# Loads of batch 0 reordered over two queues, later k and v through the Pool queue, and the expansions of k and v moved to chunks 2 and 3

## Chip, cores and metric

One core of one Trainium2 chip. The metric is the time of one execution on the device in microseconds (us), as the median of several runs. The time of a run is some 1.8 us longer than the span of its trace, in which all positions below are given.

## The reference, cut to what matters

```python
# mLSTM cell; 4 batches, 8 heads, 768 steps, head dimension 40
for t in range(S):
    m_new  = np.maximum(f[t] + m, i[t])
    f_stab = np.exp(f[t] + m - m_new);  i_stab = np.exp(i[t] - m_new);  m = m_new
    C = f_stab * C + i_stab * outer(v[t], k[t]);  n = f_stab * n + i_stab * k[t]
    y[t] = sigmoid(o[t]) * (C @ q[t]) / np.maximum(abs(n @ q[t]), 1.0)
x = y.transpose(0, 2, 1, 3).reshape(3072, 320)
# MLP, 320 -> 2048 -> 320
r = np.maximum(x @ w_in, 0.0)
out = (s * (r * r) + b) @ w_out
```

The forget gate is drawn around +3 and is added to the stabilizer m, so the weight of a step falls quickly with its number. The kernel therefore takes k and v of the first 42 steps alone, tests in each execution that this is allowed, and would branch to a full version otherwise.

## The kernel before

The 3072 tokens go in six chunks of 512. Chunk c runs its first MLP layer while the second layer of chunk c-1 runs: sixteen slots of TensorE work, into which "events" are put, that is, small steps of the attention for later chunks. `put(c, slot, step)` places one. Every chunk needs, ahead of it, q and o loaded and q cast and transposed (`qt`); `ps_h`, the state times q; the normalized result `x`; and its transpose `xt`. Chunks 2 to 5 get `qt` and `xt` by DMAs of SyncE, chunks 0 and 1 by TensorE. The state of a batch is `cn`, made from the weighted `kp` (k times the gates) and `v1` (v, cast) through `ps_cn`. The expansions `kbd` and `vbd` are block-diagonal copies of the first 42 steps' k and v, which only chunks 4 and 5 use.

```python
    def load_first(self):                              # cut
        nc.sync.dma_start(out=self.ft, in_=...)        # gates f, i
        nc.sync.dma_start(out=self.it, in_=...)
        ...
        self.load_kv(0, 1, nc.scalar)                  # k, v of batch 0
        self.load_x(0, nc.sync)                        # q, o of chunk 0
        self.load_kv(1, 2, nc.sync)
    def load_rest(self):
        nc.sync.dma_start(out=self.sc, in_=d["s"].partition_broadcast(P))
        nc.sync.dma_start(out=self.bc, in_=d["b"].partition_broadcast(P))
        self.load_kv(2, B, nc.sync)                    # k, v of batches 2 and 3
    def kw(self, bb):                                  # kp = k * gates
        nc.vector.tensor_tensor(out=self.kp[...], in0=self.k32[...], in1=self.at[...], op=ALU.mult)
    def vw(self, bb):                                  # cast of v
        self.nc.gpsimd.tensor_copy(out=self.v1[...], in_=self.v32[...])
    def ev_cn(self, bb):
        ps = self.psB.tile(..., tag="b", name="ps_cn")         # psB: one buffer, shared with ps_h
        ...                                                    # 3 matmuls, then Vector: cn = ps * mask
    def ev_kt(self, bb):
        ps = self.psO.tile(..., tag=self.spare, name="ps_kt")  # psO: one buffer per tag
        ...                                                    # 3 transposes, then Vector: kbd = ps * mask
    def ev_vr(self, bb):
        ps = self.psO.tile(..., tag=self.spare, name="ps_vr")
        ...                                                    # 3 matmuls, then Vector: vbd = ps * mask
    def start(self):                                   # cut
        self.warm(34); self.gates(); self.kw(0); self.warm(10)
        self.qcast(0, 0, nc.vector); self.qcast(0, 1, nc.scalar)
        self.ev_cn(0); self.warm(16)
        self.ev_q(0, 0); self.ev_q(0, 1, nc.vector, early=True); self.warm(12)
        self.tanh(0, 0); self.ev_h(0, 0, early=True); ...
```

`warm(n)` issues n matmuls of ones whose only purpose is to keep TensorE busy.

Of the kernel before, what the change touches and what calls it, by code (L numbers as in the profile page):

```python
# [16 lines left out]
P = 128  # L17
L = 42
# [13 lines left out]
class Short:  # L32
# [30 lines left out]
    def load_first(self):  # L63
        nc, c, d = self.nc, self.const, self.d
        self.ft = c.tile([BH, L], F32, name="ft")
        self.it = c.tile([BH, L], F32, name="it")
        nc.sync.dma_start(out=self.ft, in_=d["f"].rearrange("b h s -> (b h) s")[:, 0:L])
        nc.sync.dma_start(out=self.it, in_=d["i"].rearrange("b h s -> (b h) s")[:, 0:L])
        self.k32 = c.tile([L, BH, D], F32, name="k32")
        self.v32 = c.tile([L, BH, D], F32, name="v32")  # L70
        self.x32 = {}
        self.wi = self.keep.tile([P, 2, DFF], BF16, name="wi")
        self.wr = self.keep.tile([P, NF // 4, 2 * P], BF16, name="wr")
        self.wo = self.keep.tile([P, NF, DM], BF16, name="wo")
        self.sc = self.keep.tile([P, 1], F32, name="sc")
        self.bc = self.keep.tile([P, 1], F32, name="bc")
        self.fa = c.tile([P, S // 4], F32, name="fa")
        self.ia = c.tile([P, S // 4], F32, name="ia")
        self.load_kv(0, 1, nc.scalar)
        self.load_x(0, nc.sync)  # L80
        self.load_kv(1, 2, nc.sync)

    def load_rest(self):
        nc, d = self.nc, self.d
        nc.sync.dma_start(out=self.sc, in_=d["s"].partition_broadcast(P))
        nc.sync.dma_start(out=self.bc, in_=d["b"].partition_broadcast(P))
        self.load_kv(2, B, nc.sync)

    def load_rest2(self):
        nc, d = self.nc, self.d  # L90
# [116 lines left out]
        nc.vector.tensor_copy(out=self.tri, in_=ps)  # L207


    def kw(self, bb):  # L210
        nc = self.nc
        nc.vector.tensor_tensor(
            out=self.kp[0:L, bb, 0:H, :],
            in0=self.k32[:, bb * H : (bb + 1) * H, :],
            in1=self.at[:, bb * H : (bb + 1) * H].unsqueeze(2).to_broadcast([L, H, D]),
            op=ALU.mult,
        )
# [305 lines left out]
    def events(self):  # L523

        e = {}

        def put(c, at, step, *args):
            e.setdefault((c, at), []).append(lambda: step(*args))

        v, a = self.nc.vector, self.nc.scalar  # L530
        put(0, 0, self.qcast, 1, 0, v)
        put(0, 0, self.qcast, 1, 1, v)
        put(0, 3, self.square, 0, 0, 0)
        put(0, 4, self.ev_q, 1, 0, v)
        put(0, 4, self.ev_q, 1, 1, v, True)
        put(0, 5, self.tanh, 1, 0)
        put(0, 6, self.ev_h, 1, 0)
        put(0, 6, self.square, 0, 0, 1)
        put(0, 7, self.tanh, 1, 1)
        put(0, 10, self.ev_x, 1, 0)  # L540
        put(0, 10, self.ev_h, 1, 1)
        for n in range(2, 8):
            put(0, 9 + min(n, 6), self.square, 0, n // 2, n % 2)
        put(0, 15, self.ev_x, 1, 1)
        put(0, 15, self.bias, 0, 8)
        put(1, 0, self.make_tri)
        put(1, 1, self.kw, 2)
        put(1, 1, self.bias, 8, NF)
        put(1, 3, self.load_rest2)
        for c in range(2, 6):  # L550
            d = c - 1

            q0, r0, t0, h0, y0, q1, r1, t1, h1, y1 = {
                2: (4, 5, 6, 8, 10, 5, 6, 8, 11, 13),
                3: (-7, -6, 0, 1, 4, -6, -5, 2, 5, 8),
            }.get(c, (-11, -10, 0, 1, 4, -10, -9, 2, 5, 8))
            for at, step in (
                (q0, lambda c=c: self.qcast(c, 0, a)),
                (r0, lambda c=c: self.tr_q(c, 0)),
                (t0, lambda c=c: self.tanh(c, 0)),  # L560
                (h0, lambda c=c: self.ev_h(c, 0)),
                (y0, lambda c=c: self.tr_x(c, 0)),
                (q1, lambda c=c: self.qcast(c, 1, a)),
                (r1, lambda c=c: self.tr_q(c, 1)),
                (t1, lambda c=c: self.tanh(c, 1)),
                (h1, lambda c=c: self.ev_h(c, 1)),
                (y1, lambda c=c: self.tr_x(c, 1)),
            ):
                put(d + at // 16, at % 16, step)
            if c >= B:  # L570
                put(d - 1, 14, self.ev_s, c, 0)
                put(d, 3, self.ev_s, c, 1)
        put(1, 3, self.ev_cn, 2)
        put(1, 3, self.kw, 3)
        put(1, 6, self.ev_cn, 3)
        put(1, 2, self.ev_kt, 0)
        put(1, 4, self.ev_vr, 0)
        put(1, 7, self.ev_kt, 1)
        put(1, 9, self.ev_vr, 1)
        put(2, 9, self.ev_kt, 2)  # L580
        put(2, 10, self.ev_vr, 2)
        put(2, 11, self.ev_kt, 3)
        put(2, 12, self.ev_vr, 3)
        put(1, 14, self.load_y, 0, self.nc.sync)
        put(2, 10, self.load_y, 2, self.nc.sync)
        put(2, 1, self.flag_a)
        put(2, 3, self.flag_b)
        put(2, 7, self.flag_c)
        put(3, 9, self.flag_d)
        return e  # L590

    def start(self):

        nc = self.nc
        self.load_first()
        self.masks()
        self.vw(0)
        self.load_wi(0)
        self.load_wi(1)
        self.load_x(1, nc.gpsimd)  # L600
        self.vw(1)
        self.load_wi(2)
        self.load_wi(3)
        self.masks_late()
        for k in range(4):
            self.load_wo(k)
        self.load_rest()
        self.load_x(2, nc.gpsimd)
        self.vw(2)
        self.vw(3)  # L610
        self.load_x(3, nc.gpsimd)
        self.ps_w = self.psO.tile([P, 512], F32, tag="o0", name="ps_w")
        self.warm(34)
        self.gates()
        self.kw(0)
        self.warm(10)
        self.qcast(0, 0, nc.vector)
        self.qcast(0, 1, nc.scalar)
        self.ev_cn(0)
        self.warm(16)  # L620
        self.ev_q(0, 0)
        self.ev_q(0, 1, nc.vector, early=True)
        self.warm(12)
        self.tanh(0, 0)
        self.ev_h(0, 0, early=True)
        self.tanh(0, 1)
        self.ev_h(0, 1, early=True)
        self.warm(40)
        self.ev_x(0, 0)
        self.warm(14)  # L630

    def run(self):
        nc, tc = self.nc, self.tc
        with tc.manual_schedule():
            self.start()
            prev = None
            at = self.events()
            for c in range(6):
                for k in range(4):
                    self.spare = f"o{(k + 1) % 2}" if c > 0 else "o1"  # L640
                    if c > 0:
                        self.mm1_rem(c, k, 0)
                        self.mm1_rem(c, k, 1)
                    elif k == 0:
                        self.kw(1)
                        for a in range(2):
                            self.mm1_rem(0, 0, a, 0, N // 2)
                            self.mm1(0, 0, a, 0, N // 2)
                            if a == 0:
                                self.ev_x(0, 1)  # L650
                        self.ev_cn(1)
                        self.warm(8)
                    for a in range(2):
                        if c == 0:
                            n0 = N // 2 if k == 0 else 0
                            self.mm1_rem(c, k, a, n0)
                            self.mm1(c, k, a, n0)
                        else:
                            self.mm1(c, k, a)
                        if c > 1 or (k, a) > (0, 0) and c > 0:  # L660
                            self.square(*prev)
                        self.relu(c, k, a)
                        prev = (c, k, a)
                        for n, (f0, f1) in enumerate((((0, 3), (3, 6)), ((6, 11), (11, 16)))[a]):
                            for e in at.pop((c, 4 * k + 2 * a + n), []):
                                e()
                            if c > 0:
                                self.mm2(c - 1, k, f0, f1)
                if c == 3:
                    self.asked = nc.values_load(self.flag[0:1, 0:1], min_val=0, max_val=1)  # L670
            assert not at
            self.square(*prev)
            for tb in range(CT):
                self.mm2(5, tb, 0, NF, pool="h")
# [218 lines left out]
```

## Time and profile before

| | |
|---|---|
| median of 3 runs | 145.23 us (144.66 to 146.41) |
| span of the profiled run | 143.4 us |
| mean granted clock of TensorE | 0.991 of full speed |
| first real matmul (`hp<-xt,wr`) | 13.27 us |
| length of chunks 0, 1, 2, 3, 4 | 16.60, 23.12, 20.22, 19.14, 18.96 us |
| chunk 5 and the last second layer | 26.94 us |

The length of a chunk is the distance between the starts of the first `hp<-xt,wr` matmuls of two successive chunks, read from the timeline of TensorE. Chunk 4 has no trouble at 18.96 us, chunk 1 takes 4.16 us longer.

One row of the page is the clock granted in 40 equal slices of the span (a 9 is 90% or more of full speed). The clock's records in this trace begin at 4.15 us, and the row and the mean count the time before them as full; the warm-up matmuls of that time took about 100 ns each, against 60 ns later:

```profile
PEclk9999999999999999999999999999999999999996
```

### The profile page before, as it was taken

How to read it: one execution, taken by the hardware profiler on the slowest of the kernel's cores; microseconds unless marked ns; L12 is line 12 of the kernel's file. 1: busy time of each engine (PE TensorE's matmuls, PEld its weight loads, DVE VectorE, ACT ScalarE, POOL GpSimd, SP SyncE). 2: the span in 40 equal slices, each digit the busy share in tenths (PEclk: the TensorE clock that was granted, in tenths of full speed). 3: DMA queues.
4: the chain of work that ended last, by engine and by line, in shares of the span. 5: the costliest groups of instructions: out<-in, count | busy, mean ns of one | idle time of the engine just before them, and what ended most of it. 6: DMA issues, size and time to landing. Idle time of an engine off the chain costs nothing.

```text
span 143.4 us, 2633 instructions
## 1 busy us (share of the span) xinstructions
PE 133.4 (93%) x1009; PEld 78.9 (55%) x1009; DVE 91.7 (64%) x195; ACT 68.3 (48%) x85; POOL 20.7 (14%) x47
## 2 busy tenths in 40 slices
PE   7998999999999949999999999999999999999950
PEld 7796643456555526547555645565555454557730
DVE  6769748996769954998748984569943535244120
ACT  3362479753579316655247663465355343550000
POOL 6994959300000000000000000000000000000000
PEclk9999999999999999999999999999999999999996
DMA  3999999999151789977992365011341110111211
GB/s 50 322 189 284 263 207 197 266 314 286 54 113 46 150 169 186 176 158 160 189 200 68 97 120 139 9 50 40 63 101 46 48 48 0 46 46 46 96 51 59
DMA packets 43336, 18.45 MB, mean 129 GB/s; under 512 B 33396, under 2 KB 42452, under 8 KB 43316
## 3 DMA queue, kind: packets, MB, share of 16 engines
q1 hardware_dynamic: 37576, 11.38, 36.0%
q0 software_dynamic: 4896, 6.56, 20.9%
q10 hardware_dynamic: 844, 0.27, 0.8%
q8 instruction: 10, 0.16, 0.5%
q14 instruction: 10, 0.08, 0.2%
HBM read 13.75 MB, written 3.93 MB: 123 GB/s over the span
## 4 chain that ended last, share of the span: by engine, by line
PE 69%; DVE 5%; DMA 2%; issue 0%; SPq 0%; DVEq 0%
PE o L454 27%; PE hp L419 24%; PE hp L407 7%; PE o2t L454 6%; DMA xt<-x 2%; PE ps_h L337 1%; DVE fac L360 1%; DVE x L365 1%; PE ps_b L441 1%; DVE osb L460 1%; PE ps_kt L241 1%; PE ps_s L315 0%; DVE g L433 0%; DVE rec L358 0%; PE ps_vr L256 0%
## 5 line engine op out<-in xcount | busy, mean ns | idle before, releaser
L426 ACT ACTIVATE r<-hp 128x1024 bf16<-128x1024 f32 x48 | 49.0, 1024 | 51.4 <-PE hp L419 49.7
L454 PE MATMUL o<-wo,g 128*128 128x320 bf16 x320 | 52.6, 299 | 0.0
L419 PE MATMUL hp<-xt,wi 128*128 128x512 bf16 (+1 forms) x200 | 49.9, 372 | 0.0
L454 PEld LDWEIGHTS <-g 128*128 128x128 bf16 x384 | 36.3, 98 | 17.9 <-DVE fm L506 0.3
L433 DVE TENSOR_TENSOR g<-r 128x1024 bf16<-128x1024 bf16 x48 | 32.3, 683 | 10.7 <-ACT r L426 10.6
L419 PEld LDWEIGHTS <-wi 128*128 128x128 bf16 x200 | 17.1, 98 | 22.8 <-issue 9.8
L460 DVE SCALAR_TENSOR_TENSOR osb<-o,sc,brep 128x320 f32<-128x320 f32 x20 | 10.9, 545 | 11.2 <-PE o L454 11.0
L407 PE MATMUL hp<-xt,wr 64*128 64x512 bf16 (+1 forms) x100 | 15.6, 373 | 2.5 <-DMA xt<-x 1.8
L360 DVE SCALAR_TENSOR_TENSOR fac<-th,rec 128x640 f32<-128x640 f32 x12 | 10.5, 876 | 1.8 <-ACT th L294 0.8
L521 PE MATMUL ps_w<-ones 128*128 128x128 bf16 x134 | 10.1, 239 | 1.1 <-POOL ones L134 1.1
L365 DVE TENSOR_TENSOR x<-ps_h,fac 128x640 bf16<-128x640 f32 x12 | 9.9, 824 | 0.4
L521 PEld LDWEIGHTS <-ones 128*128 128x128 bf16 x134 | 9.1, 109 | 1.1 <-POOL ones L134 1.1
L454 PE MATMUL o2t<-wo,g 128*128 128x320 bf16 x64 | 8.9, 299 | 0.0
L407 PEld LDWEIGHTS <-wr 64*128 64x128 bf16 x100 | 3.5, 94 | 9.6 <-issue 9.0
L294 ACT ACTIVATE th<-ox 128x640 f32<-128x640 f32 x8 | 5.7, 728 | 0.5 <-DMA ox<-in_o_gate_dram 0.5
L460 DVE SCALAR_TENSOR_TENSOR osb<-o2t,sc,brep 128x320 f32<-128x320 f32 x4 | 2.2, 550 | 5.9 <-PE o2t L454 5.9
L378 ACT COPY xt<-ps_x 128x768 bf16<-128x768 bf16 x4 | 3.2, 796 | 4.0 <-PE ps_x L376 4.0
L288 ACT CAST qb<-qx 128x480 bf16<-128x480 f32 (+1 forms) x10 | 4.0, 456 | 2.1 <-DMA qx<-in_q_dram 2.1
L337 PE MATMUL ps_h<-cn,qt 120*128 120x123 bf16 (+1 forms) x60 | 4.8, 212 | 0.1
L350 DVE TENSOR_SCALAR d<-ps_h 128x16 f32<-128x16 f32 x8 | 1.4, 170 | 5.0 <-PE ps_h L337 5.0
L337 PEld LDWEIGHTS <-qt 120*128 120x128 bf16 x60 | 3.7, 98 | 1.1 <-issue 0.4
L119 POOL DMA_DIRECT2D wi<-in_moe_w_in_dram x4 | 3.1, 764 | 2.2 <-DMA wi<-in_moe_w_in_dram 2.1
(91 smaller groups left out, 82.7 us busy)
## 6 DMA issues: line engine op xcount, KB each, us to landing
out_dram<-osb SPq DMA_DIRECT2D x23, 160.0 KB, 2.0
qx<-in_q_dram POOLq DMA_DIRECT2D x3, 640.0 KB, 9.4
ox<-in_o_gate_dram POOLq DMA_DIRECT2D x3, 640.0 KB, 10.6
wo<-in_moe_w_out_dram POOLq DMA_DIRECT2D x4, 320.0 KB, 7.1
qy<-in_q_dram SPq DMA_DIRECT2D x8, 160.0 KB, 3.7
oy<-in_o_gate_dram SPq DMA_DIRECT2D x8, 160.0 KB, 3.8
wi<-in_moe_w_in_dram POOLq DMA_DIRECT2D x4, 256.0 KB, 7.9
qx<-in_q_dram SPq DMA_DIRECT2D x1, 640.0 KB, 4.5
```

The lines of the kernel that those rows point to most:

```text
L288: eng.copy(out=out, in_=in_)
L294: self.nc.scalar.activation(out=th, in_=self.src("o", c, i), func=ACT.Tanh, scale=0.5)
L337: nc.tensor.matmul(ps[:, j, g * 123 : g * 123 + w], lhsT=lhs, rhs=rhs[:, g, :, :].rearrange("k a e -> k (a e)")[:, 0:w], start=True, stop= ...
L360: nc.vector.scalar_tensor_tensor(out=fac, in0=self.th.pop((c, i))[:, :, :, :].rearrange("p j h d -> p (j h) d"), scalar=1.0, in1=rec[:, :] ...
L365: nc.vector.tensor_tensor(out=x[:, :, 0:DM].rearrange("p j (h d) -> p j h d", h=H), in0=hv[:, :, :, 0:D], in1=fac[:, :, :].rearrange("p (j ...
L407: nc.tensor.matmul(hp[:, e, n0:n1], lhsT=self.wr[64 * e : 64 * e + 64, k, a * P : (a + 1) * P], rhs=self.xt[64 * e : 64 * e + 64, t0:t1, 2 ...
L419: nc.tensor.matmul(hp[:, e, n0:n1], lhsT=self.wi[:, kt, f * P : (f + 1) * P], rhs=self.xt[:, t0:t1, kt, :], start=False, stop=(kt == 1),)
L426: self.nc.scalar.activation(out=r1, in_=self.hp.pop((c, k, a)), func=ACT.Relu)
L433: self.nc.vector.tensor_tensor(out=self.g[c][:, f : f + 3 : 2, :], in0=r1, in1=r1, op=ALU.mult)
L454: nc.tensor.matmul(self.o2[c, tb][:], lhsT=self.g[c][:, f, tb * P : (tb + 1) * P], rhs=self.wo[:, f, :], start=(f == 0), stop=(f == NF - 1),)
L460: nc.vector.scalar_tensor_tensor(out=osb, in0=self.o2.pop((c, tb)), scalar=self.sc[:, 0:1], in1=self.brep, op0=ALU.mult, op1=ALU.add)
L521: self.nc.tensor.matmul(self.ps_w[:, 0:P], lhsT=self.ones[:], rhs=self.ones[:], start=True, stop=True)
```

## The change

The intent: issue q and o of chunk 0 first, by moving the gates to Scalar's queue, where k and v of batch 0 already are; take k, v of batches 2 and 3 out of the crowded early transfers, into GpSimd's (Pool) queue; give their `kp` to GpSimd; spread the expansions, `ps_tri` and chunk 2's preparation so that Vector is free in chunk 1 and `xt` of chunk 2 is ready in time; use fewer warm-up matmuls.

```diff
-        nc.sync.dma_start(out=self.ft, ...)
-        nc.sync.dma_start(out=self.it, ...)
+        nc.scalar.dma_start(out=self.ft, ...)
+        nc.scalar.dma_start(out=self.it, ...)
     ... load_rest:
-        nc.sync.dma_start(out=self.sc, ...)
-        nc.sync.dma_start(out=self.bc, ...)
-        self.load_kv(2, B, nc.sync)
+        nc.gpsimd.dma_start(out=self.sc, ...)
+        nc.gpsimd.dma_start(out=self.bc, ...)
+        self.load_kv(2, B, nc.gpsimd)
     ... kw(self, bb, eng): eng.tensor_tensor(...) in place of nc.vector.tensor_tensor(...)
     ... events:
-        put(1, 0, self.make_tri)
-        put(1, 1, self.kw, 2)
-                2: (4, 5, 6, 8, 10, 5, 6, 8, 11, 13),
+                2: (3, 4, 5, 6, 9, 3, 4, 7, 9, 12),     # q cast, qt, tanh, ps_h, xt; twice
-        put(1, 3, self.ev_cn, 2)
-        put(1, 3, self.kw, 3)
-        put(1, 6, self.ev_cn, 3)
-        ... ev_kt and ev_vr of batches 0 and 1 at slots 2, 4, 7, 9 of chunk 1,
-            of batches 2 and 3 at slots 9 to 12 of chunk 2
+        put(1, 2, self.ev_cn, 2)
+        put(1, 7, self.ev_cn, 3)
+        put(2, 9, self.make_tri)
+        for bb, k0, v0 in ((0, 6, 7), (1, 10, 11), (2, 6, 8), (3, 10, 12)):
+            put(2 + bb // 2, k0, self.ev_kt, bb)        # batches 0, 1 in chunk 2; 2, 3 in chunk 3
+            put(2 + bb // 2, v0, self.ev_vr, bb)
     ... start:
-        self.warm(34)
+        self.warm(24)
-        self.kw(0)
-        self.warm(10)
+        self.kw(0, nc.vector)
+        self.kw(2, nc.gpsimd)
+        self.kw(3, nc.gpsimd)
+        self.warm(8)
-        self.warm(16)
-        self.ev_q(0, 0)
-        self.ev_q(0, 1, nc.vector, early=True)
-        self.warm(12)
+        self.warm(6)
+        self.ev_q(0, 0, nc.vector)
+        self.ev_q(0, 1, early=True)
+        self.warm(9)
```

After the change, line numbers from 211 to about 540 are smaller by one: L407 before is L406 after, and so on.

More of the change, by code (lines that the diff above doesn't have):

```diff
@@ L66, in load_first @@
         self.it = c.tile([BH, L], F32, name="it")
-        nc.sync.dma_start(out=self.ft, in_=d["f"].rearrange("b h s -> (b h) s")[:, 0:L])
-        nc.sync.dma_start(out=self.it, in_=d["i"].rearrange("b h s -> (b h) s")[:, 0:L])
+        nc.scalar.dma_start(out=self.ft, in_=d["f"].rearrange("b h s -> (b h) s")[:, 0:L])
+        nc.scalar.dma_start(out=self.it, in_=d["i"].rearrange("b h s -> (b h) s")[:, 0:L])
         self.k32 = c.tile([L, BH, D], F32, name="k32")
@@ L84, in load_rest @@
         nc, d = self.nc, self.d
-        nc.sync.dma_start(out=self.sc, in_=d["s"].partition_broadcast(P))
-        nc.sync.dma_start(out=self.bc, in_=d["b"].partition_broadcast(P))
-        self.load_kv(2, B, nc.sync)
+        nc.gpsimd.dma_start(out=self.sc, in_=d["s"].partition_broadcast(P))
+        nc.gpsimd.dma_start(out=self.bc, in_=d["b"].partition_broadcast(P))
+        self.load_kv(2, B, nc.gpsimd)
     def load_rest2(self):
@@ L207, in make_tri, with kw @@
         nc.vector.tensor_copy(out=self.tri, in_=ps)
-    def kw(self, bb):
-        nc = self.nc
-        nc.vector.tensor_tensor(
+    def kw(self, bb, eng):
+        eng.tensor_tensor(
             out=self.kp[0:L, bb, 0:H, :],
@@ L572, in events @@
                 put(d, 3, self.ev_s, c, 1)
-        put(1, 3, self.ev_cn, 2)
-        put(1, 3, self.kw, 3)
-        put(1, 6, self.ev_cn, 3)
-        put(1, 2, self.ev_kt, 0)
-        put(1, 4, self.ev_vr, 0)
-        put(1, 7, self.ev_kt, 1)
-        put(1, 9, self.ev_vr, 1)
-        put(2, 9, self.ev_kt, 2)
-        put(2, 10, self.ev_vr, 2)
-        put(2, 11, self.ev_kt, 3)
-        put(2, 12, self.ev_vr, 3)
+        put(1, 2, self.ev_cn, 2)
[4 more added lines that the diff above has]
+            put(2 + bb // 2, v0, self.ev_vr, bb)
         put(1, 14, self.load_y, 0, self.nc.sync)
@@ L644, in run @@
                     elif k == 0:
-                        self.kw(1)
+                        self.kw(1, nc.vector)
                         for a in range(2):
```

## The prediction

> **What bounds the kernel now.** I read the page first: busy shares, the chain that ended last, the costliest groups.
>
> ```profile
> PE 133.4 (93%) x1009; PEld 78.9 (55%) x1009; DVE 91.7 (64%) x195; ACT 68.3 (48%) x85; POOL 20.7 (14%) x47
> PE 69%; DVE 5%; DMA 2%; issue 0%; SPq 0%; DVEq 0%
> ```
>
> TensorE is the bound, and Vector has 50 us to spare on average. So the change can gain only TensorE's idle time, and loses wherever it makes TensorE wait. The list of waits names one sizeable wait of TensorE after the start:
>
> ```profile
> PE hp L407 <- DMA xt<-x: 1.8, 1, 1.8
> ```
>
> The chain in order of time shows where it sits, at the border of chunks 1 and 2. (Chunks 0 to 5 have 16 slots each: four groups k, whose slots are 4k to 4k+3; a group's last matmuls of the second layer stand in slot 4k+3.)
>
> ```profile
> 48.14 0.83 DVE x L365
> ...
> 49.19 0.47 DVE osb L460
> ...
> 49.68 0.40 SPq L472
> 50.08 0.05 issue
> 50.13 2.73 DMA xt<-x
> 52.86 0.14 issue
> 52.99 0.61 PE hp L407 x4
> ```
>
> Chunk 2's second x is ready at 49.2, but SyncE first sends group 2's output, which waits for osb; the transpose lands at 52.86. From 52.99 to 138.3 the chain is TensorE alone, but for stretches too short to see: every wait added there lengthens the kernel in full. Before chunk 1 there is the start: the first real matmul (L407) runs at 13.27, the rest is filled with warm-up matmuls.
>
> A third reading decides my prediction: how long a PSUM tile stays occupied. Pool psB has one buffer for ps_h and ps_cn; psO has one buffer per tag, and ps_kt, ps_vr, ps_fl of one group share the tag that the group's output does not use. The timelines of Vector and of TensorE in chunk 1:
>
> ```profile
> 44.50 0.82 DVE L365 TENSOR_TENSOR x<-ps_h,fac 128x640 bf16<-128x640 f32 x1
> 45.47 0.46 PE L337 MATMUL ps_h<-cn,qt 120*128 120x123 bf16 x6
> ```
>
> The second ps_h starts 0.15 us after Vector's last read of the first one (45.32): the buffer is already the limit there. And in chunk 2 Vector runs late, after two rounds of normalization and the flags:
>
> ```profile
> 60.73 0.16 DVE L350 TENSOR_SCALAR d<-ps_h 128x16 f32<-128x16 f32 x1
> ...
> 63.31 0.68 DVE L433 TENSOR_TENSOR g<-r 128x1024 bf16<-128x1024 bf16 x1
> 63.91 0.41 DVE L503 TENSOR_REDUCE fm<-ps_fl 1x2 f32<-1x256 f32 x1
> ```
>
> ```profile
> 61.24 0.84 PE L454 MATMUL o<-wo,g 128*128 128x320 bf16 x5
> 61.92 0.38 PE L498 MATMUL ps_fl<-idf,fl 128*1 128x128 f32 x2
> 62.37 0.85 PE L454 MATMUL o<-wo,g 128*128 128x320 bf16 x5
> ```
>
> TensorE writes ps_fl at 61.92, Vector reads it 2 us later, and nobody minds, since nothing reuses that buffer soon. That changes.
>
> [...] q of chunk 0 moves from 2.8 to 5.4 us, o from 5.4 to 7.7. [...] The first 34 warm-up matmuls take 3.52 us (about 100 ns each), 40 later ones 2.40 (60 ns)[...].
>
> **The change part by part.**
>
> *Start.* q and o are issued at 0.8 instead of 1.73 us, so they land some 0.9 earlier (about 5.3 and 7.9; now Scalar gets q at 6.28 and o at 8.84). But ft, it, k0, v0 all go through Scalar's queue, which delays its table load (1.28 us, now from 1.86) by about 0.9: the exponential starts near 4.1 instead of 3.84, a at 5.2, kp at 5.75. Vector's cast of q follows kp, 5.75 to 6.5 instead of 6.28 to 7.01. Then transposes, copy (now 0.56 on Vector), the 9 warm-ups, ps_h near 8.4 instead of 8.52; reciprocal and tanh end near 9.5 instead of 9.69. The chain of Vector behind it is unchanged, so the gain is about 0.2 us, not 0.9. Fewer warm-ups leave TensorE idle near 3.5 to 4.5[...]: gain between -0.8 and +1.0.
>
> *Transfers in the Pool queue.* 1344 packets of k and v leave the crowded stretch of 12 to 19 us and stand behind wo. I expect v near 26 to 30, casts, two more loads (0.93 each), then kw(2) and kw(3): kp(2) near 30 to 33.5. TensorE wants it at slot 2 of chunk 1, near 34. It fits, tightly: 0.2 us for the risk.
>
> *Chunk 1* (times from its first matmul, 29.87 before). TensorE loses ps_tri, two ps_kt, two ps_vr: 0.06 + 4 x 0.17 = 0.74 us less work. New waits: (a) ev_h(2,0) stands at slot 6, reached at 9.1. Its qt comes by a transpose that SyncE issues after group 0's output, near 7.05, and 3.0 later (39.31 to 42.3 now) it is there: 10.05, a wait of 1.0. (b) ev_cn(3), which stood before both ev_h, now stands at slot 7, 0.68 us after ps_h(2,0), and needs the same psB buffer; Vector frees it 2.5 + 0.15 us after ps_h's end: a wait of 1.95. These 2.95 us take the place of 1.84 (xt) and 0.3 (psB at 45.47). TensorE ends chunk 1 at 20.99 - 0.74 + 2.95 = 23.2; the last xt arrives between 23.1 and 23.7, as chunk 3's transposes still precede it on SyncE. Before: 23.12. So the wait for xt that the change attacks is bought back by two others: 0.0 to +0.6, taken as +0.4.
>
> *Chunk 2.* ps_kt(0) stands at slot 6, ps_vr(0) and ps_fl at slot 7, all three on one buffer, and the instruction order of the changed kernel has Vector's kbd behind ev_h(3,1) and a square. In times of now: ps_kt at 61.40, 0.68 of output matmuls, ps_vr wanted at 62.25; kbd starts at 63.91 where the reduction stands today, 0.53 long, so ps_vr at 64.5: a wait of 2.25. ps_vr 0.17, its vbd 0.25 later and 0.55 long, so ps_fl at 65.4: a wait of 0.73. Another 0.2 at slot 11. Work: +0.34 in group 1, and 0.40 for 0.62 in group 2, and 0.17 less in group 3. Sum 3.18 + 0.34 - 0.22 - 0.17 = +3.1.
>
> *Chunk 3.* Four expansions at 0.17 and a wait of 0.2 for group 1's osb, which kbd now precedes: +0.9.
>
> Sum: -0.2 + 0.2 + 0.4 + 3.1 + 0.9 = +4.4. Taken a little smaller, since Vector's backlog may be shorter than I carry over: +3.8, so 149.0 us.
>
> **Rivals.**
> 1. *The change does what it intends*: Vector is freed in chunk 1, xt comes a slot earlier, the start gains all of 0.9. For it: the 1.84 us wait and the 0.74 us of work moved. Against it: the moved work returns on TensorE, and one buffer each in psB and psO. Time: 145.23 - 1.84 - 0.9 = 142.5 at best, not quite 2%.
> 2. *GpSimd becomes the bound in chunk 1*: v lands late, kp(2) after 34. For it: its DMA issues already wait for landings (2.06 us before wi at 14.30) and DMA is about full until 36. Against it: 672 of the 160 B packets took 1.6 us on Scalar's queue. It would add 1 to 3 us to the sum, 150 to 152.
> 3. *The waits I find shrink*: the wait of chunk 1 at slot 7 only replaces the later wait for xt, and Vector reaches kbd sooner in chunk 2. Then +1 to +2: 146.2 to 147.2.
>
> **Range and chances.** The parts range from -0.8 to +1.0 at the start, -0.5 to +1.5 in chunk 1, +2.0 to +3.5 in chunk 2, +0.6 to +1.0 in chunk 3. Not all fall on one side, so 146.8 to 150.6. 2% slower is 148.13, 0.9 below my value: slower 0.70. Rival 3, or a full gain at the start, gives "same": 0.26. Over 2% faster would take more than all of TensorE's idle time after the start: 0.04.
>
> **What would show each step.** In the waits of the changed kernel: ps_vr, or L453 behind it, waiting for Vector's kbd, some 2 us, and ps_fl for vbd, 0.7 us, both in group 1 of chunk 2; ps_cn waiting about 2 us for Vector's x in chunk 1; ps_h waiting about 1 us for qt; the wait for xt under 0.6. First L406 matmul near 13.1. Kp's two multiplies on GpSimd[...] done by 33.5. I am wrong if TensorE passes slot 7 of chunk 2 without idling, if the first real matmul comes before 12.5, or if ps_cn(2) waits for GpSimd.

## More of the kernel before

Repeated runs of the kernel before lie between 144.6 and 146.9 us, but for one of 159.86 at a mean clock of 0.849. Those with a recorded clock fall into two groups: a mean of 0.989 or more took 144.59 to 145.88 us, a mean of 0.979 to 0.981 took 146.39 to 146.85. No trace of the second group was kept.

## The result, and the profile after

The changed kernel took 159.2 us (median of 4 runs, 158.95 to 160.32) against 145.09 us in the same rounds: a ratio of 1.097, with a 95% interval of 1.088 to 1.106. A ratio here and below is the mean time of one kernel's fast runs over that of the other's in the same rounds, so it is not quite the ratio of the medians quoted. The direction was predicted, the size was not: +3.8 us predicted, some +14 measured, and 159 is far outside the range.

The page of the changed kernel, its busy shares, clock row and chain:

```profile
PE 138.7 (88%) x984; PEld 80.3 (51%) x984; DVE 90.8 (58%) x193; ACT 68.3 (43%) x85; POOL 26.0 (17%) x53
PEclk9999999999995999995599999999999999999999
PE 57%; DMA 13%; DVE 10%; POOL 10%; issue 4%; ACTq 1%; SPq 1%; ACT 0%; DVEq 0%; POOLq 0%
```

TensorE has 25 instructions fewer than before and is yet busy 5.3 us longer. That points to a slower clock: three slices show a 5 where the row of before has only nines up to its last slice. TensorE's part of the chain fell from 69% to 57%: transfers, Vector and GpSimd now hold a third of the span, against 7% before.

Chunk by chunk, from the timelines of TensorE (us):

| | before | after | difference |
|---|---|---|---|
| first real matmul | 13.27 | 17.30 | +4.03 |
| chunk 0 | 16.60 | 16.40 | -0.20 |
| chunk 1 | 23.12 | 26.38 | +3.26 |
| chunk 2 | 20.22 | 26.19 | +5.97 |
| chunk 3 | 19.14 | 19.96 | +0.82 |
| chunk 4, chunk 5 and tail | 45.90 | 45.91 | 0 |
| sum | | | +13.88 |

From the list of waits after, those that matter here (total, number, longest, in us):

```profile
POOL v L219 <- DMA v<-in_v_dram: 9.7, 2, 5.4
PE ps_vr L255 <- DVE kbd L244: 2.3, 1, 2.3
PE ps_cn L225 <- DVE x L364: 2.0, 1, 2.0
PE ps_cn L225 <- POOL v L219: 2.0, 1, 2.0
DVE nm L184 <- DMA it<-in_i_gate_dram: 1.9, 1, 1.9
PE ps_h L336 <- DMA qt<-qb: 0.8, 1, 0.8
PE ps_fl L497 <- DVE vbd L260: 0.7, 1, 0.7
PE hp L406 <- DMA xt<-x: 0.6, 1, 0.6
PE ps_cn L225 <- POOL kp L211: 0.5, 1, 0.5
```

Five of these are the predicted waits, close to their predicted sizes (predicted in brackets): 2.26 for `kbd` (2.25), 1.96 for Vector's `x` (1.95), 0.82 for `qt` (1.0), 0.71 for `vbd` (0.73), 0.64 for `xt` (under 0.6). Four were not in the sum: the waits for the transfers of v and `it` and for the cast of v belong to the start, and `kp` is what the prediction named as its way to be wrong.

**The start.** The cast of v of batch 0 and the matmuls behind it, before:

```profile
3.88 0.45 POOL L220 CAST v<-v 42x320 bf16<-42x320 f32 x1 [0.36 <-DMA v<-in_v_dram]
5.58 0.38 PE L226 MATMUL ps_cn<-v,kp 128*120 128x123 bf16 x3
```

and after (start, duration, engine and line; in brackets the idle time before it and what ended it):

```profile
8.95 0.45 POOL L219 CAST v<-v 42x320 bf16<-42x320 f32 x1 [5.43 <-DMA v<-in_v_dram]
9.45 0.47 PE L225 MATMUL ps_cn<-v,kp 128*120 128x123 bf16 x3 [1.96 <-POOL v L219]
17.30 0.28 PE L406 MATMUL hp<-xt,wr 64*128 64x256 bf16 x2
```

v is usable 5 us later, `ps_cn(0)` starts 3.87 us later, and the first real matmul follows 4.03 us later. GpSimd issues the weight loads and everything else of its queue behind that cast, so all of it is late as well: the first load of `wi` is issued at 9.35 us in place of 4.28.

**The Pool queue and the two new waits of chunk 1.** TensorE after:

```profile
38.59 0.38 PE L225 MATMUL ps_cn<-v,kp 128*120 128x123 bf16 x3 [0.55 <-POOL kp L211]
40.26 0.61 PE L406 MATMUL hp<-xt,wr 64*128 64x512 bf16 x4
44.33 0.47 PE L336 MATMUL ps_h<-cn,qt 120*128 120x123 bf16 x6 [0.82 <-DMA qt<-qb]
47.45 0.48 PE L225 MATMUL ps_cn<-v,kp 128*120 128x123 bf16 x3 [1.96 <-DVE x L364]
49.19 1.04 PE L406 MATMUL hp<-xt,wr 64*128 64x512 bf16 x4
```

The last line is the surprise. The same four matmuls take 0.61 us at 40.26 and 1.04 us at 49.19, after the 1.96 us wait. The windows of the trace show why (window, its length, busy time of TensorE with the number of its instructions, of its weight loads, of Vector, Scalar and GpSimd, then the granted clock, the share of DMA and GB/s). Their borders are those of the clock's own changes, which lie 3.413 us or a multiple of it apart in the traces (in this one at 13.38, 47.51, 50.92, 71.40 and 78.23 us), and so on a grid of 3.413 us:

```profile
44.10:47.51 3.41, 1.22 (x12) 0.80 (x13) 2.43 (x6) 1.10 (x2) 0.00 (x0) 1.00 0.29 56
47.51:50.92 3.41, 3.41 (x14) 1.21 (x15) 1.72 (x4) 0.00 (x0) 0.00 (x0) 0.50 0.07 23
67.99:71.40 3.41, 1.34 (x11) 0.83 (x9) 3.19 (x7) 2.01 (x5) 0.00 (x0) 1.00 0.74 163
71.40:74.82 3.42, 2.52 (x12) 1.04 (x11) 1.23 (x4) 0.00 (x0) 0.00 (x0) 0.50 0.31 62
74.82:78.23 3.41, 3.41 (x12) 1.14 (x12) 1.15 (x2) 0.41 (x1) 0.00 (x0) 0.50 0.44 106
```

A window in which TensorE is busy only 1.22 of 3.41 us (0.36) is followed by one at half clock; the same at 67.99 (0.39), which holds most of the predicted 2.26 us wait for `kbd`. There the clock stays at half for a second window; the first one at half clock was busy 0.74. The windows from 47.51 and 74.82, busy 1.00, were each followed by full clock. This is the wait, with the Vector instruction that ended it:

```profile
71.00 0.54 DVE L244 TENSOR_TENSOR kbd<-ps_kt,bdm 120x378 bf16<-120x378 bf16 x1
71.59 0.47 PE L255 MATMUL ps_vr<-v,sel 128*126 128x123 bf16 x3 [2.26 <-DVE kbd L244]
```

The wait for `xt` of the kernel before is nearly as long (1.84 us), but a border of the grid cuts it in two: the windows that hold its halves are busy 0.77 and 0.69, and no half clock follows either:

```profile
48.52:51.94 3.42, 2.63 (x18) 1.44 (x15) 3.05 (x7) 1.68 (x2) 0.00 (x0) 1.00 0.82 178
51.94:55.35 3.41, 2.35 (x19) 1.33 (x20) 0.43 (x2) 0.74 (x1) 0.00 (x0) 1.00 0.95 167
```

So three theories had to be tested: the start is late because of the loads and not because of fewer warm-ups; two waits cost their length and half a clock window or more on top; and the Pool queue delays `kp(2)`.

### The profile page after: what moved, and what is told of

Its sections match the earlier page's. It is cut to its first block, busy times and chain, and to the rows that moved or that the text cites. A ratio compares the mean times of both kernels' runs of the same rounds, so it can differ in the third digit from the quotient of the medians.

```text
span 157.1 us, 2583 instructions
## 1 busy us (share of the span) xinstructions
PE 138.7 (88%) x984; PEld 80.3 (51%) x984; DVE 90.8 (58%) x193; ACT 68.3 (43%) x85; POOL 26.0 (17%) x53
## 3 DMA queue, kind: packets, MB, share of 16 engines
HBM read 13.75 MB, written 3.93 MB: 113 GB/s over the span
## 4 chain that ended last, share of the span: by engine, by line
PE 57%; DMA 13%; DVE 10%; POOL 10%; issue 4%; ACTq 1%; SPq 1%; ACT 0%; DVEq 0%; POOLq 0%
PE o L453 23%; PE hp L418 18%; PE hp L406 6%; PE o2t L453 6%; DMA wi<-in_moe_w_in_dram 5%; DMA v<-in_v_dram 4%; DVE fac L359 2%; DVE x L364 2%; DVE g L432 2%; DMA qt<-qb 2%; DMA xt<-x 2%; POOL qx L103 2%; POOL ox L103 2%; PE ps_h L336 1%; DVE osb L459 1%
## 5 line engine op out<-in xcount | busy, mean ns | idle before, releaser
L453 PE MATMUL o<-wo,g 128*128 128x320 bf16 x320 | 53.9, 306 | 0.0
L418 PE MATMUL hp<-xt,wi 128*128 128x512 bf16 (+1 forms) x200 | 51.1, 379 | 0.0
L453 PEld LDWEIGHTS <-g 128*128 128x128 bf16 x384 | 37.0, 99 | 18.6 <-issue 0.5
L432 DVE TENSOR_TENSOR g<-r 128x1024 bf16<-128x1024 bf16 x48 | 32.9, 694 | 12.7 <-ACT r L425 12.6
L406 PE MATMUL hp<-xt,wr 64*128 64x512 bf16 (+1 forms) x100 | 16.4, 392 | 1.3 <-DMA xt<-x 0.6
L359 DVE SCALAR_TENSOR_TENSOR fac<-th,rec 128x640 f32<-128x640 f32 x12 | 9.9, 825 | 1.8 <-ACT th L293 0.8
L520 PEld LDWEIGHTS <-ones 128*128 128x128 bf16 x109 | 8.5, 119 | 1.1 <-POOL ones L134 1.1
L406 PEld LDWEIGHTS <-wr 64*128 64x128 bf16 x100 | 3.5, 95 | 9.0 <-issue 7.1
L225 PE MATMUL ps_cn<-v,kp 128*120 128x123 bf16 x12 | 1.7, 260 | 4.5 <-DVE x L364 2.0
L230 DVE TENSOR_TENSOR cn<-ps_cn,bdm 120x369 bf16<-120x369 f32 x4 | 2.2, 546 | 3.8 <-PE ps_cn L225 3.8
```

Source lines behind the costliest of these rows:

```text
L359: nc.vector.scalar_tensor_tensor(out=fac, in0=self.th.pop((c, i))[:, :, :, :].rearrange("p j h d -> p (j h) d"), scalar=1.0, in1=rec[:, :] ...
L406: nc.tensor.matmul(hp[:, e, n0:n1], lhsT=self.wr[64 * e : 64 * e + 64, k, a * P : (a + 1) * P], rhs=self.xt[64 * e : 64 * e + 64, t0:t1, 2 ...
L418: nc.tensor.matmul(hp[:, e, n0:n1], lhsT=self.wi[:, kt, f * P : (f + 1) * P], rhs=self.xt[:, t0:t1, kt, :], start=False, stop=(kt == 1),)
L432: self.nc.vector.tensor_tensor(out=self.g[c][:, f : f + 3 : 2, :], in0=r1, in1=r1, op=ALU.mult)
L453: nc.tensor.matmul(self.o2[c, tb][:], lhsT=self.g[c][:, f, tb * P : (tb + 1) * P], rhs=self.wo[:, f, :], start=(f == 0), stop=(f == NF - 1),)
L520: self.nc.tensor.matmul(self.ps_w[:, 0:P], lhsT=self.ones[:], rhs=self.ones[:], start=True, stop=True)
```

## The experiments

All gave correct results. "First real" is the start of the first real matmul. Ratios are to the kernel before in the same rounds; the changed kernel was not run again in them, so differences to it cross rounds. By the rule of 2% the record calls `gates_only`, `warm_only`, `fill_waits` and `gates_held` unclear; what is read from them are positions in one profiled run each. How far such positions scatter: in the changed kernel and in the three runs that keep its loads and warm-ups (4, 6, 7), first real lies between 17.30 and 17.78.

**1. `undo_gates`: the changed kernel with the gates back on SyncE.**

```diff
-        nc.scalar.dma_start(out=self.ft, ...); nc.scalar.dma_start(out=self.it, ...)
+        nc.sync.dma_start(out=self.ft, ...);   nc.sync.dma_start(out=self.it, ...)
```

> The changed kernel with the loads of both gates back on SyncE's queue, ahead of q and o; all else as changed. Theory (queue order at the start: with the gates gone, q and o start first and fill the DMA engines, so that it, k and v of batch 0 land 3 to 5 us late and hold the exponential, kp, ps_cn and GpSimd's queue): the first real matmul comes back from 17.3 to about 13.3 us and the time falls by 4 us, to about 155. Rival (the 25 warm-up matmuls that were taken out leave TensorE cold, and that makes the start late): the first real matmul stays at 16 us or later, time 158 to 159.

Measured: 154.92 us (152.42 to 155.21). First real 14.31, against 17.30; cast of v at 4.00. The runs split by clock (0.960 to 0.967, and 0.983 in the fastest), so no ratio is quoted; the borders of the chunks are the evidence. The gates' queue was worth 3.0 us of the start. What remains over 13.27 may belong to the clock: the trace has a half-clock window from 7.71 to 11.13, and `all_mended` below, with the same queue for the gates and the same warm-ups, had none and started at 12.79.

**2. `gates_only`: the kernel before with only the gates moved to Scalar's queue.**

```diff
-        nc.sync.dma_start(out=self.ft, ...);   nc.sync.dma_start(out=self.it, ...)
+        nc.scalar.dma_start(out=self.ft, ...); nc.scalar.dma_start(out=self.it, ...)
```

> The kernel before with only the two gate loads moved from SyncE's to Scalar's queue. Theory of the queue order: first real matmul near 17 us instead of 13.3, v of batch 0 cast on GpSimd near 9 us, time +4 us, about 149. Rival of the cold clock: with the 34 warm-ups kept, no more than +1 us.

Measured: 150.64 us, ratio 1.037 (1.031 to 1.044). First real 18.24; chunks 1 to 5 are those of before to 0.03 us. Two lines of the change alone cost 4.97 us of the start, with all the old warm-ups in place. The cast of v waits for its transfer:

```profile
9.39 0.45 POOL L220 CAST v<-v 42x320 bf16<-42x320 f32 x1 [5.87 <-DMA v<-in_v_dram]
```

**3. `warm_only`: the kernel before with only the new warm-up counts and the swapped copies of qt.**

```diff
-        self.warm(34) ... warm(10) ... warm(16) ... warm(12)
+        self.warm(24) ... warm(8)  ... warm(6)  ... warm(9)
-        self.ev_q(0, 0); self.ev_q(0, 1, nc.vector, early=True)
+        self.ev_q(0, 0, nc.vector); self.ev_q(0, 1, early=True)
```

> The kernel before with only the fewer warm-up matmuls (24, 8, 6, 9 for 34, 10, 16, 12) and the two copies of transposed q exchanged between Vector and Scalar. Theory of the queue order: within 1 us of before. Rival of the cold clock: the granted clock comes up later than 4.2 us and the first real matmul is 2 us or more later.

Measured: 145.56 us, ratio 1.001 (0.991 to 1.011). First real 14.08, with half clock from 7.33 to 10.74, but chunk 0 then takes 16.06 in place of 16.60, and chunk 1 begins only 0.27 later. With the fewer warm-ups the clock fell in this trace (in `all_mended`, with the same warm-ups, it did not), and it cost next to nothing: the first chunk takes the delay up. What limits it instead, perhaps its transfers, was not tested.

**4. `fill_waits`: the changed kernel, TensorE kept busy in two of the waits** by matmuls with a matrix of zeros into the open sum of the output.

```diff
+    def fill(self, c, tb, n):
+        for _ in range(n):
+            self.nc.tensor.matmul(self.o2[c, tb][:], lhsT=self.zero[:], rhs=self.wo[:, 0, :], start=False, stop=False)
+        put(1, 7, self.fill, 0, 1, 14)     # ahead of ps_cn(3)
+        put(2, 7, self.fill, 1, 1, 16)     # ahead of ps_vr(0)
+        put(2, 7, self.fill, 1, 1, 5)      # ahead of ps_fl
```

> The changed kernel with matmuls by a zero matrix added to an open output sum, 14 ahead of ps_cn of batch 3 in chunk 1, 16 ahead of ps_vr and 5 ahead of ps_fl in chunk 2: TensorE works through the waits, and what it waits for is untouched. The result is the same. Theory (a stretch in which TensorE idles lets the clock fall to half for one or two windows of 3.4 us): the two half-clock stretches at 47.5 and 71.4 go, chunk 1 gets 1.5 us shorter and chunk 2 3 us shorter, total about 154.5. Rival (the waits alone cost the time, the half clock falls on work that has slack or has another cause): the time stays at 159, within 1 us.

Measured: 155.13 us, ratio 1.071 (1.062 to 1.079), so 4.1 us less than the median of the changed kernel, for *more* work on TensorE. The two windows that had been followed by half clock are now busy 0.88 and 0.96, and the clock is at 1.00 from 13.32 us to the end of the work:

```profile
44.03:47.45 3.42, 3.00 (x25) 2.07 (x25) 2.25 (x5) 1.30 (x2) 0.00 (x0) 1.00 0.30 58
67.93:71.34 3.41, 3.29 (x26) 2.07 (x24) 2.63 (x6) 0.86 (x3) 0.00 (x0) 1.00 0.88 94
```

Chunk 1 goes from 26.38 to 24.79 (-1.59), chunk 2 from 26.19 to 23.57 (-2.62). The sum, 4.21 us, is the price of the half clock; the waits themselves are still there, filled: counted from the start of their chunk, `ps_cn(3)` starts after 13.74 us (13.75 in the changed kernel) and `ps_vr(0)` after 11.51 us in both.

**5. `gates_held`: the kernel before with the gates on Scalar, but q and o kept from going early** by putting the two tiny loads of s and b ahead of them on SyncE.

```diff
-        nc.sync.dma_start(out=self.ft, ...);   nc.sync.dma_start(out=self.it, ...)
+        nc.scalar.dma_start(out=self.ft, ...); nc.scalar.dma_start(out=self.it, ...)
+        nc.sync.dma_start(out=self.sc, ...);   nc.sync.dma_start(out=self.bc, ...)   # moved up from load_rest
```

> The kernel before with the gates on Scalar's queue, as in gates_only, but with the two small loads of s and b put first on SyncE, so that q and o are issued at the same time as before the change (near 1.8 and 2.3 us). It tells apart why v of batch 0 lands at 9.3 in place of 3.5 us. Theory (q and o ahead of k and v in the DMA engines): most of the delay goes, v lands by about 5 us, first real matmul near 14, time within 1.5 us of before. Rival (being third and fourth on Scalar's queue is what delays k and v): v still lands near 9 us, time near 150.6.

Measured: 147.66 us, ratio 1.014 (1.005 to 1.024); first real 16.90 in the profiled run, which took 148.86. The cast of v starts at 7.39. That is between the theory (early q and o alone) and its rival (a later place of k and v on Scalar's queue alone). Of the 5.51 us by which the cast is late in `gates_only`, 2.00 go away when q and o start later, and 3.51 stay. Neither alone explains it.

**6. `early_cn`: the changed kernel with `ps_cn(3)` at slot 5 of chunk 1, ahead of `ps_h(2,0)`.**

```diff
-        put(1, 7, self.ev_cn, 3)
+        put(1, 5, self.ev_cn, 3)
```

> The changed kernel with ps_cn of batch 3 at slot 5 of chunk 1, ahead of ps_h(2,0), in place of slot 7 behind it. Theory (one psB buffer, and the half clock that follows the wait): the wait of 1.96 us is gone and the half-clock window behind it too, so chunk 1 takes 26.4 - 1.96 - 1.6 = 22.8 us and the total is about 155.7. Rival (the wait only stands in for a later one, for xt): chunk 1 keeps more than 25.5 us with a longer wait for xt.

Measured: 156.4 us, ratio 1.073 (1.065 to 1.082). The wait for Vector's `x` and the half clock of chunk 1 are gone: 22.83 us. But the wait for `xt` comes back (1.76 us), since the second transpose of `x` stands behind others in SyncE's program. TensorE, then SyncE:

```profile
57.07 0.60 PE L406 MATMUL hp<-xt,wr 64*128 64x512 bf16 x4 [1.76 <-DMA xt<-x]
```

```profile
48.17 2.73 SPq L391 DMA_TRANSPOSE xt<-x  x1
51.01 2.56 SPq L383 DMA_TRANSPOSE qt<-qb  x2
53.66 0.53 SPq L471 DMA_DIRECT2D out_dram<-osb  x1
54.24 1.24 SPq L391 DMA_TRANSPOSE xt<-x  x1
```

The second `x` was ready at 50.9; its transpose is issued at 54.24, behind chunk 3's two transposes of q. The half clock of chunk 2 is still there (68.89 to 75.71).

**7. `late_exp`: the changed kernel with the expansions of batches 0 and 1 at slots 9 to 12 of chunk 2**, away from the flag's `ps_fl` and from Vector's backlog.

```diff
-        put(2, 9, self.make_tri)
-        for bb, k0, v0 in ((0, 6, 7), (1, 10, 11), ...
+        put(2, 8, self.make_tri)
+        for bb, k0, v0 in ((0, 9, 10), (1, 11, 12), ...
```

> The changed kernel with the k and v expansions of batches 0 and 1 at slots 9 to 12 of chunk 2 (where those of batches 2 and 3 stood before the change) and ps_tri at slot 8. Theory (one buffer behind Vector's backlog, and the half clock after it): no wait for kbd or vbd over 0.3 us, clock full in chunk 2, chunk 2 takes 20.5 us in place of 26.2, total about 153.7. Rival (Vector has too much work in chunk 2 wherever the expansions stand): chunk 2 keeps at least 23 us.

Measured: 154.06 us, ratio 1.060 (1.049 to 1.071). Chunk 2 falls from 26.19 to 21.06 us, at full clock throughout and with no wait of TensorE over 0.23 us; chunk 1 keeps its 26.38. One to three slots' distance is worth 5.1 us.

**8. `rest_back`: the changed kernel with the loads of s, b, and k and v of batches 2 and 3 back on SyncE.** `kp(2)` and `kp(3)` stay on GpSimd.

```diff
-        nc.gpsimd.dma_start(out=self.sc, ...); nc.gpsimd.dma_start(out=self.bc, ...); self.load_kv(2, B, nc.gpsimd)
+        nc.sync.dma_start(out=self.sc, ...);   nc.sync.dma_start(out=self.bc, ...);   self.load_kv(2, B, nc.sync)
```

> The changed kernel with s, b and k, v of batches 2 and 3 on SyncE's queue again; their kp products stay on GpSimd. Theory (in the Pool queue v lands behind wo, GpSimd stands 4.3 us waiting for it, and kp(2) comes 1 us late for TensorE): GpSimd's wait and TensorE's wait for kp (0.55 us) are gone, chunk 1 is 0.6 to 1 us shorter, total about 158.3. Rival (these loads now stand in the way of q, o, wi again): the start gets later by as much, total unchanged or longer.

Measured: 157.97 us (155.88 to 159.16; two fast and two slow runs, so no ratio). `ps_cn(2)` no longer waits for GpSimd; first real is 18.26, so the start became 0.96 us later (0.48 later than the latest of the runs with the changed kernel's start). Chunk 1 falls by 2.4 us to 23.98, more than the 0.55 us of the wait for `kp`. The rest is the clock: the wait of 1.96 us for Vector's `x` is still there, but now crosses a border of the grid (45.62 to 47.58, border at 46.06), and no half-clock window follows:

```profile
46.06:49.47 3.41, 1.89 (x14) 0.93 (x15) 2.90 (x6) 0.00 (x0) 0.00 (x0) 1.00 0.02 5
```

The same wait in the same place thus costs 1.96 us here and about 3.5 in the changed kernel (1.96 plus the 1.59 of experiment 4). It was not the aim of this run, and it is the cleanest evidence that the place of the wait on the grid made the difference: the window here is busy 0.55, that of the changed kernel 0.36. The other three traces with this wait unfilled (the changed kernel, `undo_gates`, `late_exp`) have it inside one window, busy 0.36 to 0.43, and in all three the clock falls.

**9. `all_mended`: the changed kernel with the mends of 1, 6, 7 and 8 together.** What is left of the change are the fewer warm-ups, `kp` on GpSimd, chunk 2's earlier preparation and the expansions in chunks 2 and 3.

```diff
     gates on nc.sync; s, b, k, v of load_rest on nc.sync; ev_cn(3) at slot 5;
     make_tri at slot 8; expansions 0 and 1 of chunk 2 at slots 9, 10, 11, 12
```

> The changed kernel with four things taken back at once: gates on SyncE; s, b and k, v of batches 2 and 3 on SyncE; ps_cn of batch 3 at slot 5; expansions of batches 0 and 1 at slots 9 to 12 of chunk 2. Theory (the causes found, start order, Pool queue, psB buffer, psO buffer, each with its half clock, are all there is): chunk 1 under 22.5 us (a wait for xt near 1.8 remains), chunk 2 near 20.9, chunk 3 near 20, first real matmul near 14.1; total 144.5 to 146.5, that is, the 14 us are gone. Rival (something else in the change costs as well, such as the kp products on GpSimd or the earlier slots of chunk 2): 147.5 or more.

Measured: 146.43 us, ratio 1.011 (1.003 to 1.019). Of the 14 us, 1.4 are left by the medians and 0.3 by the spans of the profiled runs, so no large cause is missing from the list. Chunk 1 is 22.23 (before 23.12), chunks 2 and 3 are 0.85 and 0.82 longer: the moved work comes back where it was moved to.

**10. `spread`: a version built to beat both**: the kernel before with its loads and warm-ups, expansions at slots 9 to 12 of chunks 2 and 3, `kp(2)` and `kp(3)` on GpSimd, `ps_cn(2)` and `ps_cn(3)` at slots 2 and 4, chunk 2's preparation earlier, and chunk 3's transposes of q one slot later, so that the last `xt` of chunk 2 goes ahead of them.

```diff
-                2: (4, 5, 6, 8, 10, 5, 6, 8, 11, 13),
-                3: (-7, -6, 0, 1, 4, -6, -5, 2, 5, 8),
+                2: (3, 3, 5, 7, 9, 3, 3, 7, 9, 10),
+                3: (-7, -5, 0, 1, 4, -6, -4, 2, 5, 8),
+        put(1, 2, self.ev_cn, 2)
+        put(1, 4, self.ev_cn, 3)
+        for bb in range(4):
+            put(2 + bb // 2, 9 + 2 * (bb % 2), self.ev_kt, bb)
+            put(2 + bb // 2, 10 + 2 * (bb % 2), self.ev_vr, bb)
```

> The kernel before with what is left of the change's aim and none of its collisions: expansions spread over chunks 2 and 3 at slots 9 to 12, kp of batches 2 and 3 on GpSimd, chunk 2's casts and transposes two slots earlier and issued on SyncE ahead of the output of group 0, both ps_cn before ps_h, the second x sent to its transpose before group 2's output. All loads as before. Theory (TensorE's 1.84 us wait for xt can be removed if no PSUM buffer is reused within 2.6 us): no wait for xt, chunk 1 takes 20.3 to 20.8 in place of 23.1, chunks 2 and 3 0.7 us more together, total about 143.3, 1.2% faster than before. Rival (SyncE's queue of transposes is full in chunk 1, and the wait moves to qt of chunk 3): total 145 again.

Measured: 144.55 us (6 runs) against 145.07; ratio 0.995 (0.989 to 1.001): the same. The wait that the change set out to remove is gone: chunk 2's first matmuls stand in the timeline at 51.28 with no idle time before them.

Chunk 1 is 20.94 (-2.18). Chunk 3 pays 0.89 of it back, the start and chunk 0 0.47, chunk 2 0.07. That leaves 0.75 us in the borders, of which the spans show 0.6 (142.8 against 143.4). The idea of the change works, but is worth far less than the 1.2% expected: half a per cent by the ratio, and the interval reaches to nothing.

**11. `kv_then_gates`: the kernel before with q and o first on SyncE, and on Scalar's queue k and v first, then the gates.** It separates what 5 left open: is it the place on Scalar's queue, or q and o being early?

```diff
-        nc.sync.dma_start(out=self.ft, ...);   nc.sync.dma_start(out=self.it, ...)      # first on SyncE
+        nc.scalar.dma_start(out=self.ft, ...); nc.scalar.dma_start(out=self.it, ...)    # after k and v
```

> The kernel before with q and o first on SyncE (issued at 0.8 us, as in the change), and k, v of batch 0 first on Scalar's queue (issued at 0.8, as before the change), the gates third and fourth there. It tells apart the two halves of the delay at the start. Theory (a head start of some 1 us over q and o is what k and v lose, whichever side moves): v is cast later than 3.9 us, near 5.5 to 6.5, though it is issued as early as before, and the gates now come last, near 5 to 6, so that the first real matmul is at 15 us or later. Rival (only the place on Scalar's queue counts): v is cast at 3.9 as before.

Measured: 150.84 us, ratio 1.036 (1.023 to 1.050); first real 19.14. k and v are issued as early as before, and still the cast of v starts at 6.31 in place of 3.88; now it is the gates that come last, as Vector's first scan shows:

```profile
6.95 0.23 DVE L180 TENSOR_TENSOR_SCAN fs<-ft 32x42 f32<-32x42 f32 x1 [3.73 <-DMA ft<-in_f_gate_dram]
```

When the packets moved, from the DMA records of the traces (us, first start to last end; packets of 640, 160 and 168 bytes):

| | q, o of chunk 0 | k, v of batch 0 | gates | cast of v | first real |
|---|---|---|---|---|---|
| before | 2.83 to 7.72 | 1.87 to 3.53 | 1.83 to 2.58 | 3.88 | 13.27 |
| after | 1.93 to 7.17 | 5.26 to 7.56 | 1.87 to 4.49 | 8.95 | 17.30 |
| `gates_only` | 1.93 to 7.36 | 5.19 to 7.78 | until 4.64 | 9.39 | 18.24 |
| `gates_held` | 3.29 to 8.81 | 2.86 to 6.54 | 1.94 to 3.84 | 7.39 | 16.90 |
| `kv_then_gates` | 2.04 to 7.76 | 1.86 to 5.44 | 5.45 to 7.41 | 6.31 | 19.14 |

Once q's and o's packets move, the small loads of the other queue advance slowly in these traces: in the changed kernel k is issued at 1.74 us, q's packets start at 1.93, and k's first packet moves at 5.26. From 1.93 to 7.17 us, while q and o move there, the trace shows 278 GB/s; from 1.87 to 3.53 us in the kernel before, while k and v move, 103 GB/s. In the kernel before, the gates on SyncE gave k and v a lead of 0.96 us over q and o, and they were through in 1.66 us. With a lead of 0.43 us (`gates_held`) they take 3.68, with one of 0.18 (`kv_then_gates`) 3.58. And whichever two loads stand third and fourth on Scalar's queue behind an early q and o start only near 5.2 to 5.5 us. So both halves count here: the place in the queue and the lead over q. The change gave up both. Nor was the earlier q of use: in the changed kernel Scalar casts its part of q at 5.97 us, before at 6.28, but TensorE's transposes of q stand behind `ps_cn(0)`, which waits for v until 9.45.

## Why the prediction was wrong

By cause, with the half clock taken out through `fill_waits`:

| step of the sum | predicted | measured |
|---|---|---|
| start, with chunk 0 | -0.2 | +3.83 |
| Pool queue and chunk 1, at full clock | +0.2 and +0.4 | +1.67 |
| chunk 2, at full clock | +3.1 | +3.35 |
| chunk 3 | +0.9 | +0.82 |
| half clock after two waits | not in the sum | +4.21 |
| sum | +4.4 (taken as +3.8) | +13.88 |

**Start: wrong, in sign and size.** The failing step is "q and o are issued at 0.8 instead of 1.73 us, so they land some 0.9 earlier", with "the gain is about 0.2 us, not 0.9". I followed the time of *issue* of each load and moved its landing along. For q and o that held in part (their last packet ends at 7.17 in place of 7.72). For the loads that went behind them it failed: I delayed them by Scalar's issue times alone, 0.9 us, where v was 5 us late. I had read q's and o's packets in the trace (2.8 to 7.7 us) and did not ask what their earlier start does to the loads behind them. Experiments 2, 5 and 11 show the order and the times (the cast of v at 9.39, 7.39 and 6.31 us in place of 3.88); 1 shows that the gates' queue holds 3.0 us of the changed kernel's start. The clock in the start was at half until 13.38 us in the changed kernel (eight warm-ups in 1.03 us, 129 ns each, against 60 ns later); but `gates_only`, with all its warm-ups, has full clock only from 13.16 too, the stretch from `ps_cn(0)` to the first real matmul took 7.69 us before and 7.85 after, and 3 shows that fewer warm-ups alone cost 0.3 us by the start of chunk 1.

**Chunk 2: right.** The wait for `kbd` (2.25 predicted, 2.26 measured) and for `vbd` (0.73, 0.71), worked out from Vector's backlog over a single PSUM buffer, are the best part of the prediction. `late_exp` confirms the cause: the same work one to three slots later costs 5.1 us less, of which 2.62 are the half clock (experiment 4).

**Half clock: missing.** This is the second failing step, and it sits in "every wait added there lengthens the kernel in full". Two of them lengthened it by more. I had read a slow stretch only in the warm-up (100 ns a matmul, later 60), and had in hand two predicted waits of about 2 us, as against a kernel before whose one wait of that size after the start (1.84 us) did not show in its clock row. With 4.21 us this error is as large as that of the start.

**Chunk 1: the mechanism right, the size off.** The waits for Vector's `x` (1.95, 1.96) and `qt` (1.0, 0.82) came as worked out, and "bought back by two others" is what happened. Over the +0.6 of the two terms stand 1.07 us: 0.35 more for `kp(2)`, some 0.3 more for `xt`, 0.2 less for `qt`. Of the remaining 0.6 us, some 0.5 are waits that are listed too short, since the profile models the ends of matmuls: by the starts, the waits for `kp`, `qt` and `x` are each 0.16 to 0.17 us longer. (`ps_cn` starts 1.57 us after the four `hp` matmuls at 37.02; without a wait the next starts 0.86 after such a group. That is 0.71 us, listed as 0.55.)

**Pool queue: the falsifier that fired.** "It fits, tightly: 0.2 us for the risk" failed: `kp(2)` was ready near 38.5 rather than by 33.5. Part of it is the start again: GpSimd's queue begins behind the cast of v, 5 us late. The last part is that GpSimd then stood 4.31 us waiting for v of batches 2 and 3 in its own queue. The multiply itself is no cause: 0.71 and 1.20 us for the two. A reading was loose too: of the 1344 packets that I placed at 12 to 19 us, half had moved by 11.87.

**Chunk 3: right** (0.9 and 0.82).

**Rivals.** Rival 1 got its effect in chunk 1 only in `spread`, where it gave -2.18 us there and 0.5% in all, not told apart from nothing. Rival 2 was half right, with 0.55 us in place of 1 to 3. Rival 3, that the waits shrink, fell. The reduction from 4.4 to 3.8 "since Vector's backlog may be shorter" was unfounded: the backlog was exactly as carried over.

**What stays open.** Why q's and o's stream goes ahead: the runs show the order and the times, not the rule, and do not tell apart whether the small loads' packets waited in the DMA engines or were handed to them late. For the clock, after the start, windows busy 0.36 and 0.39 (changed kernel), 0.34 (`early_cn`, from 65.47 us) and 0.43 (`late_exp`, from 44.54) were followed by half clock, and windows busy 0.46 (`gates_held`, from 53.48), 0.49 (`early_cn`, from 55.23) and 0.55 (`rest_back`, from 46.06) were not. In the start, with many small matmuls, windows busy 0.59 (`warm_only`, 3.92 to 7.33) and 0.67 (`undo_gates`, 4.30 to 7.71) were followed by half clock, so these shares do not fit one line with the later ones. Nor do the returns: full clock came after 0.80 in `warm_only` (0.51 to 3.92), and not after 0.87 in `gates_held` (2.28 to 5.69). What sets the clock was not shown.

## What to carry to other kernels

When a change issues one load earlier, ask which small loads lose their lead, and follow the landing of the small ones, not the issue of the large one: here q and o were issued 0.9 us earlier and v of batch 0 was cast 5.07 us later. A wait of TensorE of some 2 us cost about its own length twice here (1.96 us and 1.59 for the half clock, 2.26 and 2.62): read the granted clock in the window after it, and fill a wait that can't be removed with something to do, which took 4.21 us off in `fill_waits`. With a single PSUM buffer TensorE waited here for the reader's whole backlog (2.26 us for `kbd`, 1.96 for `x`) and 0.05 to 0.15 us more from the reader's end to the next write (71.54 to 71.59 for `kbd`, 45.32 to 45.47 for `ps_h` before); the two waits could be worked out from the trace of the kernel before to within 0.1 us.
